# Strided and local attention before a bilinear feed-forward layer: local heads from batch 2 on with probabilities as weights, rows turned by DMA

## The chip, the core and the metric

The kernel runs on one core of one Trainium2 chip. The metric is the device time of one execution in microseconds (us). Before the change the median of three executions is 328.6 us (328.22 to 328.73). Times inside the kernel are taken from one profiled execution and count from the start of its span.

## What is computed

Eight batches of eight heads, 576 positions of 64 numbers each. Heads 0 to 3 attend locally (the last 32 positions), heads 4 to 7 attend to every 32nd earlier position. The head outputs of a position lie side by side and make one row of 512 numbers; the 4608 rows go through a bilinear feed-forward layer.

```python
mask_local = (rel >= 0) & (rel < stride)
mask_strided = (rel >= 0) & (pos[None, :] % stride == pos[:, None] % stride)
masks = np.stack([mask_local if h < H // 2 else mask_strided for h in range(H)], axis=0)
scores = np.where(masks[None, :, :, :], scores, -1000000000.0)
scores = scores - np.max(scores, axis=-1, keepdims=True)
attn = np.exp(scores)
attn = attn / (np.sum(attn, axis=-1, keepdims=True) + 1e-09)
return np.matmul(attn, v).astype(np.float32)
...
x = np.ascontiguousarray(attn_out.transpose(0, 2, 1, 3)).reshape(B * S, H * D)
...
a = x @ w_a
b = x @ w_b
return (a * b @ w_out).astype(np.float32)
```

## The kernel before

**The feed-forward layer sets the rhythm.** The rows are cut into nine tiles of 512. A tile has 16 slots, numbered through as `16 t + n`. In slots 0 to 11 (`ffn_ab`) TensorE forms 128 columns of `x @ w_a` and `x @ w_b`, eight matmuls of 512 columns (L603); ScalarE copies the first product out of PSUM (L620) and VectorE multiplies the two into `pf` (L623, L625). In slots 12 to 15 the tile is multiplied with `w_out`: plainly in tiles 0 and 1 (`ffn_y`, L755, a ScalarE copy at L764), and in tiles 2 to 8 by a scheme of seven half-size products (`ffn_ys` and `y_plan`, L691). There the products follow one another in `Y_ORDER`, six matmuls for each entry; the three PSUM banks X, Y and Z are accumulated on by several products, and ScalarE copies a bank out in between (`y_post`, L668). Thus product "1" is copied out of bank X before product "6" goes on adding to that bank; between them TensorE has the two entries of product "7", twelve matmuls.

**The left operand.** `xT` holds the rows turned, 128 features on the partitions in four chunks (chunks 0 and 1 are the local heads, 2 and 3 the strided ones), for four batches in a ring. Tile t reads the first columns of batch t, so batch b has to stand in `xT` when slot 16 b begins. In its first slot a tile takes chunks 0, 1 and 2 first and chunk 3 last (tile 1 leaves chunk 1 for last).

**Attention is woven in between.** The steps of batch b from 1 on are put at slots by the tables `STEPS` (batches 1 and 2), `LATER` and `IN_Y` (3 to 7), counted from slot 16 (b - 1). `S` is a unit of scores (L385), its exponential on ScalarE (L406) and its mask on VectorE (L424). `V` is a unit of outputs. A batch has eight units, 0 to 3 local and 4 to 7 strided; a unit is half of the positions of two heads. What stands at a whole number n runs behind the slot's own work, what stands at n - 0.5 runs in its middle. The order of every engine's instructions is this written order.

**Two forms of V.** Batches 0 and 1 use the probabilities as weights and the values, with a column of ones behind them, as the moving operand (`V_p`, L463). That gives rows with positions on the partitions; VectorE takes the reciprocal of the sums (`V_r`, L471) and multiplies (`V_n`, L486), and TensorE turns the rows by transposes (`step_X`). From batch 2 on (`FIRST_D`) `step_VT` uses the values as weights, with 64 columns of ones behind them, and the probabilities as the moving operand (L507). This gives the outputs turned already, and the sums in 64 partitions; ScalarE takes the logarithm (L516) and the exponential of its negative (L517), and VectorE multiplies straight into `xT` (L521 local, L523 strided). The ones are set by `fill_v`, a memset on GpSimd.

**Queues.** Loads go over GpSimd's queue. SyncE's queue has the stores of the results and the transfers that place the turned q and k of the next batch (`step_D`, L341 and L345). ScalarE's queue issues one transfer in all, a last piece of the output (L657).

Of the kernel before, what the change touches and what calls it, by code (L numbers as in the profile page):

```python
# [8 lines left out]
BF16 = mybir.dt.bfloat16  # L9
# [5 lines left out]
FIRST_D = 2  # L15
RL = 6
RS = 8
# [4 lines left out]
LW = 96  # L22
# [8 lines left out]
def kernel(  # L31
# [10 lines left out]
    nc = tc.nc  # L42
    B, H, S, D = q.shape
# [9 lines left out]
    HL = H // 2  # L53
# [5 lines left out]
    sb = ctx.enter_context(tc.tile_pool(name="sb", bufs=3))  # L59
    fsb = ctx.enter_context(tc.tile_pool(name="ffn", bufs=2))  # L60
    pst = ctx.enter_context(tc.tile_pool(name="pst", bufs=1, space=bass.MemoryType.PSUM))
    dram = ctx.enter_context(tc.tile_pool(name="dram", bufs=2, space=bass.MemoryType.DRAM))
# [18 lines left out]
    vl_buf = [const.tile([128, HL * 6, VW], BF16, name=f"vl{i}") for i in range(2)]  # L81
# [76 lines left out]
    XR = 4  # L158
    xT = const.tile([128, KD, XR * S], BF16)
# [11 lines left out]
    def fast_w(n, gs):  # L171
        a, b = ((wov[:, 0, 1], wov[:, 0, 0]), (wov[:, 1, 1], wf[:, 0]), (wov[:, 1, 1], wov[:, 0, 1]),
                (wov[:, 1, 0], wf[:, 1]))[n]
        nc.vector.tensor_tensor(wf[:, n, gs], a[:, gs], b[:, gs], op=ALU.subtract)
# [3 lines left out]
    def blocks(nm, z):  # L178
        z = int(z)
        return sb.tile([128, 2, (S, RS * GP)[z]], BF16, tag=f"t{nm}{z}", name=f"t{nm}{z}", bufs=1)  # L180
# [84 lines left out]
    def by_row(t):  # L265
        return t.rearrange("p (r h d) -> p h r d", h=2, d=D)

    def pair_up(nm, c):

        if (nm, c) == ("k", 1):  # L270
            t = shared[1][:96, -RL * 128:]
        else:
            t = blocks(*{"k0": "q0", "q0": "q1", "q1": "k0"}[f"{nm}{c}"])
            t = t.rearrange("p h n -> p (h n)")[:96, :RL * 128]
        nc.vector.tensor_copy(by_row(t), nats[1, nm, False][:, 2 * c:2 * c + 2])
        paired[1, nm, c] = t.rearrange("p (r m) -> p r m", r=RL)
# [85 lines left out]
    def unit(u):  # L362

        c, half = u // 2, u % 2
        return (c, half, 128, LW, 3) if c < 2 else (c, half, NP, NP, 4)
# [68 lines left out]
    xn = {}  # L434

    def V_p(b, u):
        c, half, M, n, G = unit(u)
        p = ps.pop((b, u))
        if b == 0:

            o = psum4["o"].tile([128, 512], F32, tag="o", name="o")
            if c < 2:
                of = o[:, :2 * G * (D + 1)].rearrange("p (j g e) -> p j g e", j=2, e=D + 1)
                sm = of[:, :, :, D:]
            else:
                of = o.rearrange("p (j g e) -> p j g e", j=2, e=D)
                sm = psum4["sum"].tile([128, 2, 4, 1], F32, tag="sum", name="sum")
        else:
            o = psum4["o"].tile([128, 2, 512], F32, tag="o", name="o")
            of = o[:, :, :G * (D + 1)].rearrange("p j (g e) -> p j g e", e=D + 1)  # L450
            sm = of[:, :, :, D:]
        for i in range(G):
            for j in range(2):
                if c < 2:
                    vt = vl_buf[b % 2][:, (2 * c + j) * 6 + 3 * half + i, 0:D + 1]
                elif b == 0:
                    r = 2 * i + j
                    vt = nats[0, "v", c - 2][:NP, half, r * D:(r + 1) * D]
                else:
                    vt = vs_buf[b % 2][:, 2 * (c - 2) + half, 2 * i + j, 0:D + 1]  # L460
                w = vt.shape[1]
                pt = p_cols(b, p, j, i, n, 128)[:M]
                nc.tensor.matmul(of[:, j, i, :w], lhsT=pt, rhs=vt, start=True, stop=True)  # L463
                if b == 0 and c >= 2:
                    nc.tensor.matmul(sm[:, j, i], lhsT=pt, rhs=vl_buf[0][:M, 0, D:D + 1], start=True, stop=True)
        held[b, "o", u] = of[:n, :, :, :D], sm[:n]

    def V_r(b, u):
        c, half, M, n, G = unit(u)
        rc = sb.tile([128, 2, 4], F32, tag="rc", name="rc")  # L470
        nc.vector.reciprocal(rc[:n, :, :G].unsqueeze(3), held[b, "o", u][1])  # L471
        held[b, "rc", u] = rc

    def V_n(b, u):
        c, half, M, n, G = unit(u)
        ov, _ = held.pop((b, "o", u))
        rc = held.pop((b, "rc", u))
        if (b, c // 2) not in xn:
            x = sb.tile([128, RS * 4 * D], BF16, tag="xr", name="xr", bufs=2)
            xn[b, c // 2] = x[:n, :S // n * 4 * D].rearrange("p (g h d) -> p g h d", h=4, d=D)  # L480
        x = xn[b, c // 2][:, :, 2 * (c % 2):2 * (c % 2) + 2, :]
        if c < 2 or b >= FIRST_D:
            dst = x[:, G * half:G * half + G].rearrange("p g j d -> p j g d")
        else:
            dst = x[:, :, half, :].rearrange("p (g j) d -> p j g d", j=2)
        nc.vector.tensor_mul(dst, ov, rc[:n, :, :G].unsqueeze(3).to_broadcast([n, 2, G, D]))  # L486

    def step_V(b, u):
        if b >= FIRST_D:
            step_VT(b, u)  # L490
            return
        V_p(b, u)
        V_r(b, u)
        V_n(b, u)

    def step_VT(b, u):

        c, half, M, n, G = unit(u)
        p = ps.pop((b, u))
        o = psum4["o"].tile([128, 2, 512], F32, tag="o", name="o")  # L500
        for i in range(G):
            for j in range(2):
                if c < 2:
                    vt = vl_buf[b % 2][:, (2 * c + j) * 6 + 3 * half + i]
                else:
                    vt = vs_buf[b % 2][:, 2 * (c - 2) + j, 4 * half + i]
                nc.tensor.matmul(o[:, j, i * n:(i + 1) * n], lhsT=vt, rhs=p_cols(b, p, j, i, n, n)[:M], start=True, stop=True)  # L507

        r = sb.tile([128, RS * 4 * D], BF16, tag="xr", name="xr", bufs=2)[:64, :4 * W].bitcast(F32)
        r = r.rearrange("p (j w) -> p j w", j=2)  # L510
        if c < 2:
            sums = o[64:, :, :W]
        else:

            sums, r = (t.rearrange(e, p=NP) for t, e in ((o[64:, :, :W], "d j (g p) -> d j p g"), (r, "d j (p g) -> d j p g")))
        nc.scalar.activation(r, sums, ACT.Ln)  # L516
        nc.scalar.activation(r, r, ACT.Exp, scale=-1.0)  # L517
        for j in range(2):
            dst = xT[64 * j:64 * j + 64, c, S * (b % XR):S * (b % XR + 1)]
            if c < 2:  # L520
                nc.vector.tensor_mul(dst[:, W * half:W * (half + 1)], o[:64, j, :W], r[:, j])  # L521
            else:
                nc.vector.tensor_mul(dst.rearrange("d (p r) -> d p r", r=RS)[:, :, G * half:G * (half + 1)],  # L523
                                     o[:64, j, :W].rearrange("d (g p) -> d p g", p=NP), r[:, j])
# [21 lines left out]
    def step_X(b, c):  # L546
# [15 lines left out]
    STEPS = {1: {5.5: "Tk2", 6: "Tq2", 7: "S4 Tk3", 7.5: "S5", 8: "Tq3", 8.5: "V4", 9: "S6 V5 Pk0", 9.5: "S7 Pq0",  # L562
# [4 lines left out]
    LATER = {-1: "S0", 0: "S1", 1: "V0", 2: "S2", 3: "V1", 4: "S3", 5: "V2", 6: "S4", 7: "V3", 8: "S5", 9: "V4", 10: "S6",  # L567
             11: "V5"}
    IN_Y = {2: "S7", 6: "V6", 11: "V7"}
    FN = {"Tk": step_Tk, "Tq": step_Tq, "S": step_S, "V": step_V, "X": step_X, "W": lambda b, n: fast_w(n, slice(0, 3)),  # L570
          "s": S_px, "m": S_m, "L": lead_vl, "Pk": lambda b, c: pair_up("k", c), "Pq": lambda b, c: pair_up("q", c),
          "Z": lambda b, n: zero_qz(0, nc.vector, ((1, 1),)), "D": lambda b, n: step_D(FIRST_D, 0, "k", n)}

    def run(b, slot):
# [209 lines left out]
    with tc.manual_schedule(engines={ENG.PE, ENG.SP, ENG.Pool, ENG.DVE, ENG.Activation}):  # L784
# [11 lines left out]
        for x, src in ((raw[0], k), (raw[1], q)):  # L796
            nc.sync.dma_start(out=x[:96].rearrange("p (h r d) -> p h r d", h=2, d=D),
                              in_=src[0, 0:2].rearrange("h (p r) d -> p h r d", r=RL))
# [62 lines left out]
        for b in range(1, B):  # L861
            for pos, names in (STEPS.get(b) or {16 * (b - 1) + x: n for x, n in LATER.items()}).items():
                steps.setdefault(pos, []).append((b, names.split()))
# [6 lines left out]
        def do(i, fn, *args):  # L870
            at.setdefault(i, []).append(lambda: fn(*args))

        soon = {}
        for t in FAST_Y[:-1]:
            soon[16 * t + 10] = [lambda t=t: fast_s(t, 2, slice(4, 6))]
            soon[16 * t + 11] = [lambda t=t, n=n: fast_s(t, n, slice(4, 6)) for n in (0, 1)]
        do(0, fill_v, vl_buf[0])
        do(0, fill_v, vs_buf[0])
        for c in range(4):
            do(0, load_wo, c)  # L880
# [25 lines left out]
        for i, jz in ((2, (0, 0)), (3, (1, 0)), (0, (0, 1))):  # L906
            do(i, zero_qz, 0, nc.vector, (jz,))
        do(14, rezero, 1)
        do(27, fill_v, vl_buf[1])
        do(28, fill_v, vs_buf[1])  # L910
        for n, slot in enumerate((16, 16, 19, 20)):
            do(slot, fast_w, n, slice(3, 6))
# [50 lines left out]
```

## Time and profile before

| what | value |
|---|---|
| median of three executions | 328.6 us |
| the profiled execution | 328.45 us |
| its span in the trace | 326.6 us |
| granted TensorE clock | 1.0 throughout |
| local units in the form of L507 | 24 (6 batches of 4), 144 matmuls of 96 columns |
| ScalarE's Ln and Exp (L516, L517) for all 48 units | 31.1 us and 32.8 us |
| VectorE's multiplies of the local units (L521) | 48 of 450 ns |
| GpSimd's memsets of the values' ones (L109) | 2 of 1.4 us and 2 of 1.8 us |

Busy times of an engine say little where instructions overlap: a matmul's record holds its latency, while the next one begins much sooner. The pace is read from the start of one group of matmuls to the start of the next.

### The profile page before, as it was taken

The numbers are of one execution on the slowest core, as the hardware profiler recorded it, in microseconds if no ns is written. First come the engines' busy times: TensorE is split into PE (matmuls) and PEld (weight loads), VectorE is DVE, ScalarE is ACT, GpSimd is POOL, SyncE is SP. The second block draws the span as 40 slices with busy tenths as digits, with TensorE's granted clock in tenths as the row PEclk, the third lists the DMA queues.
The fourth block names the chain that finished last, engine by engine and source line by source line (L and its number), as shares of the span: only waits on it lengthen the run. The fifth ranks groups of instructions, "written<-read, shape, count | busy, mean of one in ns | idle before, by whom it ended". The sixth has DMA issues, their size and how long they took to land.

```text
span 326.6 us, 7290 instructions
## 1 busy us (share of the span) xinstructions
PE 321.0 (98%) x2624; PEld 205.4 (63%) x2624; DVE 251.0 (77%) x530; ACT 210.1 (64%) x345; POOL 150.9 (46%) x280
## 2 busy tenths in 40 slices
PE   8999999999999999999999999999999999999994
PEld 6754555455555587557999885569555954584474
DVE  6766888889778989799879988998878645626652
ACT  6763775478778876887677767786777743323341
POOL 8845839599866554664475346643011001100000
PEclk9999999999999999999999999999999999999999
DMA  9999999999999799989898959897032040004004
GB/s 154 149 204 202 204 184 181 167 178 134 140 209 119 87 95 83 95 221 101 82 84 202 130 63 102 160 172 83 20 90 101 2 129 0 2 0 131 0 0 130
DMA packets 98724, 37.48 MB, mean 115 GB/s; under 512 B 76672, under 2 KB 95744, under 8 KB 98688
## 3 DMA queue, kind: packets, MB, share of 16 engines
q0 software_dynamic: 85968, 19.48, 64.2%
q1 hardware_dynamic: 12576, 17.47, 18.4%
q8 instruction: 21, 0.34, 0.4%
q14 instruction: 15, 0.12, 0.1%
q10 hardware_dynamic: 144, 0.07, 0.1%
HBM read 39.51 MB, written 9.44 MB: 150 GB/s over the span
## 4 chain that ended last, share of the span: by engine, by line
PE 93%; POOL 2%; DMA 2%; DVE 1%; ACT 0%; issue 0%; POOLq 0%
PE mm L603 55%; PE mm L691 17%; PE mm L755 6%; PE st L385 4%; PE o L507 4%; DMA vl<-in_v_dram 2%; PE mm L720 2%; POOL shared L196 1%; PE o L463 1%; PE end L720 1%; PE ab L603 1%; PE tp L532 1%; POOL vl L224 0%; PE tp L286 0%; PE tp L295 0%
## 5 line engine op out<-in xcount | busy, mean ns | idle before, releaser
L603 PE MATMUL mm<-xT,wa_sb 128*128 128x512 bf16 (+1 forms) x472 | 110.3, 357 | 0.0
L603 PE MATMUL mm<-xT,wb_sb 128*128 128x512 bf16 (+1 forms) x472 | 110.3, 357 | 0.0
L620 ACT COPY a_sb<-mm 128x512 f32<-128x512 f32 x106 | 62.1, 586 | 45.4 <-PE mm L603 44.7
L929 POOL CAST pace<-pf 1x1 f32<-1x1 bf16 x87 | 24.5, 281 | 113.4 <-DVE pf L623 108.5
L603 PEld LDWEIGHTS <-wb_sb 128*128 128x128 bf16 x480 | 46.4, 98 | 44.3 <-DMA wb_sb<-in_moe_w_b_dram 0.5
L623 DVE TENSOR_TENSOR pf<-a_sb,mm 128x512 bf16<-128x512 f32 x84 | 57.0, 679 | 18.6 <-PE mm L603 14.2
L603 PEld LDWEIGHTS <-wa_sb 128*128 128x128 bf16 x480 | 44.0, 98 | 31.2
L516 ACT ACTIVATE xr<-o 64x576 f32<-64x576 f32 x48 | 31.1, 648 | 22.6 <-PE o L507 22.3
L406 ACT ACTIVATE p<-st 72x576 bf16<-72x576 f32 (+1 forms) x56 | 36.4, 650 | 4.0 <-PE st L385 3.6
L517 ACT ACTIVATE xr<-xr 64x576 f32<-64x576 f32 x48 | 32.8, 683 | 1.5
L521 DVE TENSOR_TENSOR xT<-o,xr 64x288 bf16<-64x288 f32 x48 | 21.6, 450 | 13.3 <-ACT xr L517 12.6
L523 DVE TENSOR_TENSOR xT<-o,xr 64x288 bf16<-64x288 f32 x48 | 21.4, 446 | 11.7 <-ACT xr L517 11.1
L691 PEld LDWEIGHTS <-ps 128*128 128x128 bf16 x288 | 28.0, 98 | 3.1
L668 ACT COPY y_sb<-mm 128x512 f32<-128x512 f32 (+1 forms) x28 | 15.6, 556 | 17.9 <-PE mm L691 14.5
L691 PE MATMUL mm<-wf,ps 128*128 128x256 bf16 x216 | 25.5, 273 | 0.0
L755 PE MATMUL mm<-wo_sb,pf 128*128 128x512 bf16 x96 | 23.4, 379 | 0.0
L242 POOL DMA_DIRECT2D vs<-in_v_dram x24 | 19.6, 818 | 5.0 <-PE mm L691 2.4
L691 PEld LDWEIGHTS <-pf 128*128 128x128 bf16 x216 | 20.3, 98 | 2.5 <-issue 0.2
L691 PE MATMUL mm<-wo_sb,pf 128*128 128x256 bf16 x144 | 18.5, 273 | 0.1
L625 DVE TENSOR_TENSOR pf<-a_sb,mm 128x512 bf16<-128x512 f32 x22 | 14.9, 677 | 4.5 <-ACT a_sb L620 2.7
L211 POOL DMA_DIRECT2D kl<-in_k_dram x24 | 16.0, 665 | 5.1 <-issue 3.2
L211 POOL DMA_DIRECT2D ql<-in_q_dram x24 | 16.0, 665 | 5.0 <-DMA wo_sb<-in_moe_w_out_dram 3.9
(146 smaller groups left out, 453.6 us busy)
## 6 DMA issues: line engine op xcount, KB each, us to landing
out_dram<-y_sb SPq DMA_DIRECT2D x12, 512.0 KB, 5.5
out_dram<-y_sb SPq DMA_DIRECT2D x11, 256.0 KB, 3.4
vl<-in_v_dram POOLq DMA_DIRECT2D x6, 384.0 KB, 6.7
kl<-in_k_dram POOLq DMA_DIRECT2D x24, 72.0 KB, 2.9
ql<-in_q_dram POOLq DMA_DIRECT2D x24, 72.0 KB, 3.1
vs<-in_v_dram POOLq DMA_DIRECT2D x24, 72.0 KB, 3.4
wo_sb<-in_moe_w_out_dram POOLq DMA_DIRECT2D x4, 384.0 KB, 9.3
natk<-in_k_dram POOLq DMA_DIRECT2D x20, 72.0 KB, 3.3
```

The costliest lines, as they stand in the source:

```text
L211: nc.gpsimd.dma_start(out=t[32 * h:32 * h + 32], in_=src[b, h].rearrange("(i y) d -> y i d", y=32))
L406: nc.scalar.activation(p_flat(p)[:M, :2 * W].rearrange("p (i n) -> p i n", n=2 * n), st[:M].rearrange("p a (i n) -> p (a i) n", n=256)[:, ...
L516: nc.scalar.activation(r, sums, ACT.Ln)
L517: nc.scalar.activation(r, r, ACT.Exp, scale=-1.0)
L521: nc.vector.tensor_mul(dst[:, W * half:W * (half + 1)], o[:64, j, :W], r[:, j])
L523: nc.vector.tensor_mul(dst.rearrange("d (p r) -> d p r", r=RS)[:, :, G * half:G * (half + 1)], o[:64, j, :W].rearrange("d (g p) -> d p g", ...
L603: nc.tensor.matmul(ps_[:, c0:c0 + n], lhsT=w[:, kk, 128 * f:128 * (f + 1)], rhs=xT[:, kk, x0:x0 + n], start=(kk == first and c0 == 0), sto ...
L620: nc.scalar.copy(a_sb, ab[0])
L623: nc.vector.tensor_mul(pf[:, f, :].rearrange("p (i a s) -> p a i s", i=2, s=16), halves(a_sb), halves(ab[1]))
L691: nc.tensor.matmul(bank[b][:, q], lhsT=lhs(g, q), rhs=rhs(g), start=k in "172" and q == 0 and g == 0, stop=g == FG - 1, skip_group_check=True)
L755: nc.tensor.matmul(ybank[j], lhsT=pf[:, f, 128 * j:128 * (j + 1)], rhs=wo_sb[:, f], start=(f == 0), stop=(f == FD - 1))
L929: nc.gpsimd.tensor_copy(pace, done)
```

## The change

For the local units (u below 4) from batch 2 on, the outputs are made as in batches 0 and 1: `V_p`, `V_r` and `V_n`, into a tile `xl` of 96 partitions with 6 rows of 256 numbers each. The rows of a batch then go to a scratch tensor in DRAM by one transfer (`rows_out`, step "O"), which ScalarE's queue issues for batch 2 and SyncE's queue for the later ones. Two transfers with transposition read it back, one for each chunk of 128 features, into `xT` (`rows_in`, step "I"); ScalarE's queue issues both. `O0` stands at slot 27 for batch 2 and at 16 (b - 1) + 7 for the others; `I0` and `I1` stand at 29 and 29.5 (behind V6 of that place), and at 16 (b - 1) + 11 (behind V5) and 11.5. The strided units keep `step_VT`. The columns of ones of the local values are no longer filled beyond the single one that `consts` sets.

```diff
@@ -476,7 +476,10 @@
         if (b, c // 2) not in xn:
-            x = sb.tile([128, RS * 4 * D], BF16, tag="xr", name="xr", bufs=2)
+            if b >= FIRST_D:
+                x = sb.tile([128, RL * 4 * D], BF16, tag="xl", name="xl", bufs=1)
+            else:
+                x = sb.tile([128, RS * 4 * D], BF16, tag="xr", name="xr", bufs=2)
@@ -486,12 +489,25 @@
-        if b >= FIRST_D:
+        if b >= FIRST_D and u >= 4:
             step_VT(b, u)
             return
         V_p(b, u)
         V_r(b, u)
         V_n(b, u)
+
+    scratch = {}
+
+    def rows_out(b, _):
+
+        scratch[b] = dram.tile([S, HL * D], BF16, tag="xd", name="xd")
+        (nc.scalar if b == FIRST_D else nc.sync).dma_start(out=scratch[b].rearrange("(g p) e -> p g e", p=LW),
+                                                           in_=xn.pop((b, 0)).rearrange("p g h d -> p g (h d)"))
+
+    def rows_in(b, c):
+
+        nc.scalar.dma_start(out=xT[:, c, S * (b % XR):S * (b % XR + 1)], in_=scratch[b][:, 128 * c:128 * (c + 1)],
+                            transpose=True)
@@ -562,13 +578,13 @@
-             2: {20: "S0", 20.5: "S1", 21.5: "V0", 22: "S2", 23: "V1", 23.5: "S3", 24.5: "V2", 25: "S4", 26: "V3", 26.5: "S5",
-                 27.5: "V4", 28: "S6", 28.5: "V5", 29: "S7", 29.5: "V6", 30.5: "V7"}}
-    LATER = {-1: "S0", 0: "S1", 1: "V0", 2: "S2", 3: "V1", 4: "S3", 5: "V2", 6: "S4", 7: "V3", 8: "S5", 9: "V4", 10: "S6",
-             11: "V5"}
+             2: {20: "S0", 20.5: "S1", 21.5: "V0", 22: "S2", 23: "V1", 23.5: "S3", 24.5: "V2", 25: "S4", 26: "V3", 26.5: "S5", 27: "O0",
+                 27.5: "V4", 28: "S6", 28.5: "V5", 29: "S7 I0", 29.5: "V6 I1", 30.5: "V7"}}
+    LATER = {-1: "S0", 0: "S1", 1: "V0", 2: "S2", 3: "V1", 4: "S3", 5: "V2", 6: "S4", 7: "V3 O0", 8: "S5", 9: "V4", 10: "S6",
+             11: "V5 I0", 11.5: "I1"}
@@ -874,7 +890,6 @@
-        do(0, fill_v, vl_buf[0])
         do(0, fill_v, vs_buf[0])
...
-        do(27, fill_v, vl_buf[1])
         do(28, fill_v, vs_buf[1])
```

More of the change, by code (lines that the diff above doesn't have):

```diff
@@ L564 @@
                  12.6: "S1", 12.75: "L0 X2", 13: "s2 X3 V0 m2 L1 W3", 13.5: "V1 S3", 14: "V2 X0", 14.5: "V3 D1", 15: "X1"},
[2 rows of a table removed]
-    LATER = {-1: "S0", 0: "S1", 1: "V0", 2: "S2", 3: "V1", 4: "S3", 5: "V2", 6: "S4", 7: "V3", 8: "S5", 9: "V4", 10: "S6",
-             11: "V5"}
[2 rows of a table added]
+    LATER = {-1: "S0", 0: "S1", 1: "V0", 2: "S2", 3: "V1", 4: "S3", 5: "V2", 6: "S4", 7: "V3 O0", 8: "S5", 9: "V4", 10: "S6",
+             11: "V5 I0", 11.5: "I1"}
     IN_Y = {2: "S7", 6: "V6", 11: "V7"}
     FN = {"Tk": step_Tk, "Tq": step_Tq, "S": step_S, "V": step_V, "X": step_X, "W": lambda b, n: fast_w(n, slice(0, 3)),
-          "s": S_px, "m": S_m, "L": lead_vl, "Pk": lambda b, c: pair_up("k", c), "Pq": lambda b, c: pair_up("q", c),
+          "s": S_px, "m": S_m, "L": lead_vl, "O": rows_out, "I": rows_in, "Pk": lambda b, c: pair_up("k", c), "Pq": lambda b, c: pair_up("q", c),
           "Z": lambda b, n: zero_qz(0, nc.vector, ((1, 1),)), "D": lambda b, n: step_D(FIRST_D, 0, "k", n)}
```

## The prediction

> **What bounds the kernel now.** I read the page's busy shares and its chain of waits first, then the order of time of TensorE and ScalarE around the places that the change touches, and last the rows of transfers. The first two say who holds the time:
>
> ```profile
> PE 321.0 (98%) x2624; PEld 205.4 (63%) x2624; DVE 251.0 (77%) x530; ACT 210.1 (64%) x345; POOL 150.9 (46%) x280
> PE 93%; POOL 2%; DMA 2%; DVE 1%; ACT 0%; issue 0%; POOLq 0%
> ```
>
> TensorE is the bound. From about 20 us on, its groups follow one another without a hole worth naming, so the time changes in two ways only: TensorE has less to do, or something now keeps it waiting. ScalarE is 0% of the chain: work taken from it is worth nothing by itself, but a delay put on it is worth whatever TensorE then waits.
>
> **Removed from TensorE.** In the order of time, the start of a group against the start of the next gives its pace. The old form, then the form that the change puts in its place (from batch 1, which has it already):
>
> ```profile
> 68.79 0.42 PE L507 MATMUL o<-p,vl 128*128 128x96 bf16 x6
> 69.05 1.03 PE L603 MATMUL mm<-xT,wb_sb 128*128 128x512 bf16 x4
> ```
>
> ```profile
> 51.78 0.34 PE L463 MATMUL o<-vl,p 128*128 128x65 bf16 x6
> 51.96 0.41 PE L385 MATMUL st<-qz1l,kT1l 128*128 128x192 bf16 x3
> ```
>
> A unit of six matmuls takes 0.26 us with 96 moving columns and 0.18 to 0.20 us with 65 (four groups: 0.19, 0.18, 0.20, 0.18; mean 0.19). The gain is 0.07 us a unit, times 24 units: **-1.7 us**, all on the path. If the weight loads, which are now the masked probabilities, came late, nothing of it would be left; a unit of scores stands at least two slots (some 4 us) ahead of its outputs, so I keep the 1.7, with 0 as its other end.
>
> **Removed from ScalarE and VectorE.** Per local unit ScalarE loses a Ln and an Exp (0.65 + 0.68 us), 24 x 1.33 = 32 us in all. VectorE has 2 x 0.45 us replaced by these two:
>
> ```profile
> L486 DVE TENSOR_TENSOR xr<-o,rc 96x384 bf16<-96x384 f32 x8 | 4.3, 547 | 0.2
> L471 DVE RECIPROCAL rc<-o 96x6 f32<-96x6 f32 x8 | 1.5, 190 | 2.4 <-PE o L463 2.3
> ```
>
> That is 0.74 for 0.90 us, 24 x 0.16 = 4 us less. I cost both at nothing: TensorE covers them, having waited for neither. The one stall that I see at the head of a product stage (184.35 to 184.65 us, behind L623 of VectorE) might shrink; it is worth 0.3 us at most. GpSimd's two memsets of 1.4 us on the values also go; only the pacing and the loads stand behind them, and the loads have slack: nothing.
>
> **Added: the rows out.** One transfer of 576 rows of 512 bytes a batch. For batch 2, ScalarE issues it at slot 27, between its copy that ends at 81.03 us and its Ln at 82.06 us; an issue of 0.66 us fits this idle time. For the others SyncE issues it at slot 7. In tile 4, the tightest, the k transfers ahead of it end at 179.8 us and SyncE is next busy at 183.72 us, so it goes out at about 180 us and lands by 183.4 us with the 3.4 us of the 256 KB row below; ScalarE wants it at 185.9 us. Cover 2.5 us; no cost.
>
> **Added: two transposing transfers a batch, on ScalarE's queue.** This is the step that matters. The trace has no transfer with transposition. The nearest rows are these, the first with the duration of an issue, the others with the time to landing:
>
> ```profile
> L657 ACTq DMA_DIRECT2D out_dram<-y_sb x1: 655/655/655, 322.5 to 322.5; - x1
> ```
>
> ```profile
> out_dram<-y_sb SPq DMA_DIRECT2D x11, 256.0 KB, 3.4
> ...
> shared<-in_k_dram POOLq DMA_DIRECT2D x5, 144.0 KB, 5.6
> ...
> out_dram<-y_sb SPq DMA_DIRECT2D x1, 128.0 KB, 2.6
> ```
>
> Let T be the time for which one such issue keeps ScalarE, and L its time to landing (one moves 576 x 128 x 2 bytes, 144 KB). L lies between 2.6 and 5.6 us by these rows; I take 4.4, about half way between 3.4 and 5.6, since loads and q and k transfers run beside it. T is bounded below by 0.66, and above by the whole landing, 5.6, if the queue takes a transposition no faster than it is carried out. The nearest row is the issue on the same queue, and a transposition can hardly have fewer pieces than a plain copy: I take **T = 1.0**, that row and half as much again.
>
> What is queued behind them in batches 3 to 7? `I0` follows V5's Exp, and `I1` (middle of slot 12) comes before the copy of product "1", so both issues stand in one row ahead of that copy. Tile 2, ScalarE and TensorE in order of time:
>
> ```profile
> 116.43 0.65 ACT L516 ACTIVATE xr<-o 64x576 f32<-64x576 f32 x1 [0.54 <-PE o L507]
> 117.11 0.68 ACT L517 ACTIVATE xr<-xr 64x576 f32<-64x576 f32 x1
> 117.82 0.59 ACT L668 COPY y_sb<-mm 128x512 f32<-128x512 f32 x1
> 118.30 0.65 ACT L406 ACTIVATE p<-st 72x576 bf16<-72x576 f32 x1
> ```
>
> ```profile
> 117.79 2.78 PE L691 MATMUL mm<-wf,ps 128*128 128x256 bf16 x24
> 120.41 0.43 PE L507 MATMUL o<-p,vs 72*128 72x72 bf16 x8
> ```
>
> The copy starts 30 ns after the Exp, without idle time. TensorE's 24 matmuls take 2.62 us, 0.109 each; the first twelve are product "7" and the thirteenth adds to the bank that the copy reads: 117.79 + 1.31 = 119.10. The copy ends at 118.41. The cover is 0.7 us, and TensorE waits 2T - 0.7. Tiles 3, 5 and 6 show the same gap; in tile 4 the copy has another 0.25 us of idle time, so 0.97 there. Behind it, S7's exponential (until 118.95) has to pass VectorE's mask before V6's matmuls at 120.41: 118.95 + 0.45 leaves 1.0, less strict than the first. Sum for five batches: 10T - (4 x 0.7 + 0.97) = 10T - 3.8, at T = 1.0 **+6.2 us**; 2.8 at T = 0.66 and 52 at T = 5.6.
>
> Do they land in time? `I1` is issued at 117.8 + T; tile 3 wants chunk 1 at about 126.8 + (2T - 0.7), over 9 us later at T = 1. Hidden up to L of about 9.
>
> **Batch 2 has less room.** Its issues stand around V6 in the plain product stage of tile 1:
>
> ```profile
> 87.04 0.65 ACT L406 ACTIVATE p<-st 72x576 bf16<-72x576 f32 x1
> 88.27 0.65 ACT L516 ACTIVATE xr<-o 64x576 f32<-64x576 f32 x1 [0.58 <-PE o L507]
> 88.95 0.68 ACT L517 ACTIVATE xr<-xr 64x576 f32<-64x576 f32 x1
> ...
> 92.47 0.81 PE L603 MATMUL mm<-xT,wa_sb 128*128 128x512 bf16 x3
> ```
>
> The last of these lines is TensorE's first group of tile 2. `I0` goes at 87.69 and holds ScalarE to 88.69, V6's Ln and Exp end 0.4 us later than before, at 90.05; then `I1`. With L = 4.4 it lands at 94.45. TensorE wants chunk 1 at 92.47 + 0.22 = 92.69: **+1.8 us**, between 0 (T 0.66, L 2.6: it lands at 92.3) and 3.0 (L 5.6).
>
> **The sum.** -1.7 + 6.2 + 1.8 = +6.3 us on the profiled execution of 328.45 us (it lies 0.15 under the median, its span at 326.6): **334.7 us**.
>
> One rule speaks against the change. The Trainium skill (VectorE: DVE Perf Modes, "The three transpose paths") puts a 128x128 bf16 transposition at 1309 ns by DMA against 390 ns on TensorE. No row here shows the first. As an estimate from that page, 4.5 such blocks a transfer would be 5.9 us, both in a row 11.8; then chunk 1 would also come late in batches 3 to 7, by some 2 us each, and the sum would be near 347 us. The same skill (DMA: Bandwidth & Descriptors, "Latency and other measured facts") gives transposing transfers 261 GB/s, by which 144 KB are an estimated 0.6 us and the landing would be like a plain copy's; the forecast is nearer to this one.
>
> **The rivals.**
>
> *The issue is hidden (other side).* ScalarE's sequencer might issue while the Exp ahead is still running, since the transfers do not depend on it. Then 0.68 us of the two issues are covered, and with the 0.7 of the copy nothing is lost up to T = 0.69. For it: nothing in the two transfers waits for the Exp. Against: the only issue on ScalarE here, at 322.52, begins after the activation before it has ended (322.23), which decides nothing. Batch 2 would then be late by 0 to 1.3. Time 328.45 - 1.7 = 326.8, or up to 328.1 with batch 2 late.
>
> *The issue is long.* If the queue builds the transposition piece by piece, ScalarE becomes the bound at the head of every product stage. From T = 1.5 on I count it as this case: T = 2.5 gives 25 - 3.8 + 3 - 1.7 = +22.5, 351 us; the bound of 5.6 gives over 380. For it: 576 rows against the 128 of an output store. Against: SyncE's issues take about 0.6 us whatever their shape.
>
> *All landings late.* At T = 1 this decides from L over 9: at L = 12, 5 x 2.7 more, and batch 2 late by 90.05 + 12 - 92.69 = 9.4: 328.45 - 1.7 + 6.2 + 13.5 + 9.4 = 356 us. Against: no transfer of this size takes over 5.6 us beside the same loads.
>
> *The change does not do what it says*: the units keep 0.26 us, because weight loads set the pace. That alone would bring 336.4 us; the four groups of batch 1 speak against it.
>
> **Chances and range.** Forecast (T from 0.7 to 1.5, including the units' rival) 0.48; issue hidden 0.25; issue long 0.19; landings late 0.08. The forecast's own range is 330 to 341 (T 0.7 to 1.5, batch 2 between 0 and 3, rounded). The range over the cases is 326.6 to 350; above it lie half of the long issues and of the late landings, below it hardly anything. A difference of under 0.2% (0.66 us) can't be told from no change. Faster than that needs the hidden issue and batch 2 in time: 0.16. Within it: 0.09. Slower: 0.75.
>
> **What would show it.** Each step has a place in the changed profile: groups of L463 at 0.19 us from batch 2 on; ScalarE's issue row of the transposing transfers with T; a hole of TensorE of 2T - 0.7 before the third entry of product stage of tiles 2 to 6, put down to ScalarE's L668 copy; a wait of the first L603 of tile 2 for a transfer into `xT`. The forecast is wrong if TensorE shows no hole at the third entry, or if its holes are at the heads of tiles 3 to 7.

## The result, and the profile after

The changed kernel takes **339.36 us** (median of four executions, 337.54 to 340.98) against 328.67 us (328.22 to 329.6) before it on the same chip: a ratio of 1.032, with an interval of 1.026 to 1.038. It is slower. The predicted time was 334.7 us and its range 326.6 to 350. The profiled execution is the fastest of the four: 337.54 us, with a span of 335.7, so that between the two profiled spans (326.6 before) 9.1 us have to be found.

Line numbers are 16 higher from L507 on (`V_n`'s L486 is L489): the tile's matmuls L603 are L619 now, the product stage's L691 is L707, its copy L668 is L684; `V`'s L507, L516 and L517 are L523, L532 and L533. The transfers into `xT` are L509.

First the page's busy shares and its chain of waits, as before:

```profile
PE 318.6 (95%) x2597; PEld 203.2 (61%) x2624; DVE 246.5 (73%) x530; ACT 178.0 (53%) x297; POOL 149.1 (44%) x278
PE 81%; DMA 7%; ACTq 3%; DVE 3%; ACT 3%; issue 2%; SPq 1%; DVEq 0%
```

ScalarE gave up 32.1 us of busy time (210.1 to 178.0) and the kernel became longer. TensorE's share of the chain fell from 93% to 81%, and what came in is above all DMA, from 2% to 7%; ScalarE's queue, ScalarE and VectorE have 3% each. Where TensorE stood still is told by the list of what it waited for (the engine and line that waited, what ended the wait, us in total, how often, the longest):

```profile
PE mm L707 <- ACT y_sb L684: 7.2, 5, 1.9
PE o L523 <- DVE xT L539: 2.2, 1, 2.2
...
PE mm L619 <- DMA xT<-xd: 0.6, 1, 0.6
PE tp L286 <- ACT shared L837: 0.4, 1, 0.4
```

None of these four is in the same list of the kernel before. Five waits for the copy of product "1" are the predicted holes; the next two belong to batch 2. The last lies at the kernel's start; L286 waits there in `b3` and `b3_one` below as well, which leave batch 2 alone, and for 0.6 us in `v_only`, which has none of the transfers. So the transfers don't explain it.

**The holes.** Tile 2 in order of time, TensorE and then ScalarE, after the change (start, duration, engine and line, what it does; in brackets the idle time before it and what ended that):

```profile
120.15 1.47 PE L707 MATMUL mm<-wf,ps 128*128 128x256 bf16 x12
122.92 1.47 PE L707 MATMUL mm<-wf,ps 128*128 128x256 bf16 x12 [1.29 <-ACT y_sb L684]
```

```profile
119.47 0.68 ACT L533 ACTIVATE xr<-xr 64x576 f32<-64x576 f32 x1
119.53 2.63 ACTq L509 DMA_TRANSPOSE xT<-xd  x2
122.28 0.59 ACT L684 COPY y_sb<-mm 128x512 f32<-128x512 f32 x1 [2.13 <-PE mm L707]
```

The first twelve matmuls are product "7"; the next should begin 12 x 0.109 = 1.31 us later, at 121.46, and begin at 122.92, 1.46 late (1.29 of it is idle, since the record of the first twelve holds their latency). ScalarE explains it: its two issues stand in one row from 119.53 to 122.16, and the copy follows at 122.28. The issues begin 0.06 us after the Exp has *begun*, not after it has ended. The bracket behind the copy names TensorE, which had been done for long: ScalarE was held by the issues, and that is read from the line above, not from the bracket. Tiles 3 to 6 have idle times of 1.38, 1.48, 1.88 and 1.14 at the same place.

In tiles 3 to 5 the first issue comes later behind the Exp's start, because `I0` waits there until its rows have landed in DRAM. Tile 4, and the row of the transfers out on SyncE's queue (KB each, median us from issue to landing):

```profile
190.04 0.68 ACT L533 ACTIVATE xr<-xr 64x576 f32<-64x576 f32 x1
190.43 2.75 ACTq L509 DMA_TRANSPOSE xT<-xd  x2
```

```profile
xd<-xl SPq DMA_DIRECT2D x5, 288.0 KB, 6.4
```

The rows of tile 4 were sent at 183.95 us and landed 6.4 us later, at 190.35. `I0` went at 190.43, 0.39 us behind the Exp's start in place of 0.06. In tiles 3 and 5 it went 0.23 and 0.57 us behind it, after landings of 6.6 and 7.2 us; in tile 6 again 0.07. Over the three tiles this is 1.0 us, and they are the ones with the longest holes.

The line's own row gives an issue its price (duration in ns, least, median, most):

```profile
L509 ACTq DMA_TRANSPOSE xT<-xd x12: 1144/1234/1377, 88.9 to 262.6; - x12
...
DMA to landing us min/median/max: 2.7/4.7/5.7
```

**Batch 2.** ScalarE from 86 to 93 us:

```profile
86.63 0.65 ACT L406 ACTIVATE p<-st 72x576 bf16<-72x576 f32 x1
88.90 1.22 ACTq L509 DMA_TRANSPOSE xT<-xd  x1
90.22 0.65 ACT L532 ACTIVATE xr<-o 64x576 f32<-64x576 f32 x1 [2.94 <-issue]
...
92.02 1.19 ACTq L509 DMA_TRANSPOSE xT<-xd  x1
```

An issue that needs nothing more stands idle on ScalarE from 87.28 (the end of L406) to 88.90, and the second, behind V6's Exp, until 92.02. TensorE pays twice:

```profile
92.58 0.43 PE L523 MATMUL o<-p,vs 72*128 72x72 bf16 x8 [2.16 <-DVE xT L539]
...
95.33 0.38 PE L619 MATMUL mm<-xT,wa_sb 128*128 128x512 bf16 x1 [0.56 <-DMA xT<-xd]
```

First V7 waits until V6 has passed ScalarE and VectorE, then tile 2 waits for chunk 1. What the second issue waited for is in the chain of waits, followed back from there (start, duration, what):

```profile
86.05 5.95 DMA kT1l<-tk
...
92.02 3.28 DMA xT<-xd
```

It is a transfer of SyncE's queue, issued at 86.05, that places the turned k of batch 3: data with which batch 2's rows have nothing to do. In the built program the transfers of SyncE's and ScalarE's queues share eight completion counters in turn, in the order in which they are written, and a transfer is not sent before the last one on its counter has landed. The trace's records of the issues, which name the counters, bear this out. `I0` waits for the counter of a transfer into `qz1l` that was issued at 83.50 and landed at 88.82, 0.08 us before `I0` went; `I1` shares with the one shown, which landed at 91.99. The rows were not what `I0` waited for: sent at 80.29, they had landed by 84.8.

**The gain** is there too. The unit of L507 shown before took 0.26 us; in its place:

```profile
68.67 0.34 PE L463 MATMUL o<-vl,p 128*128 128x65 bf16 x6
68.85 1.03 PE L619 MATMUL mm<-xT,wb_sb 128*128 128x512 bf16 x4
```

It is 0.18 us from start to start, 0.08 less. The account of the 9.1 us: the holes 7.2 idle and some 0.17 more each by the starts, 8.0; batch 2, 2.16 + 0.56 = 2.7; the start 0.4; less 1.7 of shorter outputs: 9.4.

### The profile page after: what moved, and what is told of

The parts are those of the page before. It is cut to its first block, busy times and chain, and to the rows that moved or that the text cites. A ratio compares the mean times of both kernels' runs of the same rounds, so it can differ in the third digit from the quotient of the medians.

```text
span 335.7 us, 7209 instructions
## 1 busy us (share of the span) xinstructions
PE 318.6 (95%) x2597; PEld 203.2 (61%) x2624; DVE 246.5 (73%) x530; ACT 178.0 (53%) x297; POOL 149.1 (44%) x278
## 4 chain that ended last, share of the span: by engine, by line
PE 81%; DMA 7%; ACTq 3%; DVE 3%; ACT 3%; issue 2%; SPq 1%; DVEq 0%
PE mm L619 51%; PE mm L707 13%; PE st L385 3%; PE mm L771 3%; ACTq L509 3%; PE o L463 2%; DMA kT1l<-tk 2%; DMA xT<-xd 2%; PE mm L736 2%; PE o L523 2%; DMA raw<-in_q_dram 1%; PE end L736 1%; DMA qz0s<-tq 1%; SPq L345 1%; DMA qz0l<-tq 1%
## 5 line engine op out<-in xcount | busy, mean ns | idle before, releaser
L619 PE MATMUL mm<-xT,wb_sb 128*128 128x512 bf16 (+1 forms) x468 | 109.9, 357 | 0.5
L619 PE MATMUL mm<-xT,wa_sb 128*128 128x512 bf16 (+1 forms) x453 | 108.5, 356 | 1.3 <-DMA xT<-xd 0.6
L619 PEld LDWEIGHTS <-wb_sb 128*128 128x128 bf16 x480 | 46.3, 98 | 44.2 <-DMA wb_sb<-in_moe_w_b_dram 0.3
L619 PEld LDWEIGHTS <-wa_sb 128*128 128x128 bf16 x480 | 43.6, 98 | 32.1 <-issue 0.8
L406 ACT ACTIVATE p<-st 72x576 bf16<-72x576 f32 (+1 forms) x56 | 36.4, 650 | 19.0 <-PE st L385 18.8
L539 DVE TENSOR_TENSOR xT<-o,xr 64x288 bf16<-64x288 f32 x48 | 21.4, 446 | 19.6 <-ACT xr L533 19.2
L707 PEld LDWEIGHTS <-ps 128*128 128x128 bf16 x288 | 28.0, 98 | 11.1 <-issue 8.0
L707 PE MATMUL mm<-wf,ps 128*128 128x256 bf16 x216 | 26.3, 272 | 7.2 <-ACT y_sb L684 7.2
L684 ACT COPY y_sb<-mm 128x512 f32<-128x512 f32 (+1 forms) x28 | 15.5, 554 | 26.4 <-PE mm L707 16.3
L771 PE MATMUL mm<-wo_sb,pf 128*128 128x512 bf16 x93 | 23.1, 379 | 0.2
L532 ACT ACTIVATE xr<-o 64x576 f32<-64x576 f32 x24 | 15.5, 647 | 12.0 <-PE o L523 9.0
L707 PEld LDWEIGHTS <-pf 128*128 128x128 bf16 x216 | 20.3, 98 | 2.6 <-issue 0.2
L424 DVE TENSOR_TENSOR p<-p,mask_s 72x576 int16<-72x576 int16 x28 | 12.5, 448 | 8.4 <-ACT p L406 8.3
L707 PE MATMUL mm<-wo_sb,pf 128*128 128x256 bf16 x144 | 18.5, 273 | 0.1
L653 DVE TENSOR_TENSOR ps<-pf 128x512 bf16<-128x512 bf16 (+1 forms) x48 | 17.7, 380 | 0.4
```

What stands on the lines that cost most here:

```text
L406: nc.scalar.activation(p_flat(p)[:M, :2 * W].rearrange("p (i n) -> p i n", n=2 * n), st[:M].rearrange("p a (i n) -> p (a i) n", n=256)[:, ...
L619: nc.tensor.matmul(ps_[:, c0:c0 + n], lhsT=w[:, kk, 128 * f:128 * (f + 1)], rhs=xT[:, kk, x0:x0 + n], start=(kk == first and c0 == 0), sto ...
L653: nc.vector.tensor_tensor(s[:, n], a, b, op=op)
L707: nc.tensor.matmul(bank[b][:, q], lhsT=lhs(g, q), rhs=rhs(g), start=k in "172" and q == 0 and g == 0, stop=g == FG - 1, skip_group_check=True)
L771: nc.tensor.matmul(ybank[j], lhsT=pf[:, f, 128 * j:128 * (j + 1)], rhs=wo_sb[:, f], start=(f == 0), stop=(f == FD - 1))
```

## The experiments

The theory after the result: the holes of tiles 2 to 6 are the price of two issues ahead of one copy, fixed for each issue, and batch 2 loses by waits of its own. Rivals: the price goes with the rows or bytes; the matter is the landings; or something else of the change (the rows out, VectorE's new work) costs. Each run has its own runs of the kernel before beside it; ratios are against these.

### Without the rows coming in, and without the rows going out either

`no_in` leaves out the two transfers into `xT` (the local chunks of batches 2 to 7 then aren't renewed; half of them is set to zero once), `v_only` the rows out as well.

```diff
-                 27.5: "V4", 28: "S6", 28.5: "V5", 29: "S7 I0", 29.5: "V6 I1", 30.5: "V7"}}
+                 27.5: "V4", 28: "S6", 28.5: "V5", 29: "S7", 29.5: "V6", 30.5: "V7"}}
...
-             11: "V5 I0", 11.5: "I1"}
+             11: "V5"}
```

In `v_only` the steps `O0` go too.

> The changed kernel without the two transposing transfers; the rows still go out to DRAM. The local heads' chunks of the left operand are not renewed from batch 2 on (a memset on GpSimd at slot 10 fills the ring's places of batches 2 and 3 once). Theory A (the two issues hold ScalarE ahead of the copy of product 1, and batch 2's V6 and landing wait on them; nothing else costs): all holes vanish and the shorter outputs remain, 328.6 - 1.7 = 326.9 us. Theory B (the rows' way out, or VectorE's new steps, cost too): above 328.6 us. Theory C (the shorter moving operand saves nothing in place): 328.6 us.

> As the run without the transposing transfers, and without the transfer to DRAM as well: the outputs in their new form alone. The local heads' chunks are not renewed from batch 2 on. Theory A: 326.9 us, the same as with the rows going out within 0.3 us, since the transfer out is covered. Theory B with the price in the transfer out: lower than the run with it by that price.

`no_in`: 327.2 us against 328.77, ratio 0.996 (0.9945 to 0.998). `v_only`: 327.65, ratio 0.996 (0.9945 to 0.998). So the shorter outputs are worth 1.6 us by the medians of `no_in` and 1.7 by its span (324.9 against 326.6). `v_only` shows less, 1.1 and 0.7 (its span is 325.9); two waits ahead of batch 2 that `no_in` doesn't have (0.6 us at L286, 0.4 for `wb_sb`) are 1.0 us of its span. The rows out by themselves cost nothing that can be told, and all of the loss comes with the two transfers into `xT`. The list of TensorE's waits of `no_in` has none of the four lines above.

### I1 at another place

`i1_late` issues `I1` of batches 3 to 7 behind the copy of product "7", `i1_v6` behind V6 of the product stage.

```diff
-             11: "V5 I0", 11.5: "I1"}
-    IN_Y = {2: "S7", 6: "V6", 11: "V7"}
+             11: "V5 I0"}
+    IN_Y = {2: "S7", 4: "I1", 6: "V6", 11: "V7"}
```

For `i1_v6` the last line is `IN_Y = {2: "S7", 6: "V6 I1", 11: "V7"}`.

> The changed kernel with I1 of batches 3 to 7 moved from the middle of slot 12 to behind the copy of product 7 (behind the fourth entry of the product stage). Theory A: one issue of 1.24 us ahead of the copy of product 1 is covered by the Exp (0.62) and by the 0.7 of TensorE's twelve matmuls, the other by ScalarE's idle time behind the copy of product 7. The five holes (7.2 us by the waits, some 8 by the starts) go, batch 2's 3 us stay: 339.4 - 8 = 331.4 us. Theory B (the transfers' landings or their load on the queues set the loss, wherever they are issued): 339 us.

> I1 of batches 3 to 7 behind V6 of the product stage, still later than in the run with I1 behind product 7. Theory D: there two holes stayed (tiles 4 and 5, 1.2 and 1.7 us) because I1 waited until a q transfer landed that shares its counter; by V6's Exp it has landed, and the issue lies beside this Exp and ScalarE's idle 0.87 us behind it. All five holes go: 335.3 - 3.6 = 331.7 us, batch 2's 3 us staying. If the issue's length alone made those two holes: 335 us. Price of lateness: if I1 lands over 3 to 4 us after its issue, tiles 3 to 7 wait at their head for it, up to 1 us each.

`i1_late` took 335.33 us against 328.77, ratio 1.020 (1.019 to 1.022): better than the change, but 4 us more than expected. The holes of tiles 2, 3 and 6 were gone; tiles 4 and 5 kept 1.20 and 1.68 us. The chain of waits of `i1_late` in tile 4 says why (start, duration, what):

```profile
190.06 3.02 DMA qz0l<-tq
...
193.10 1.23 ACTq L509
```

The copy before the issue had ended at 191.62. The issue stood until 193.10, for a transfer of SyncE's queue that places q, and the next copy stood behind it: the wait of batch 2 again, at a new place. The two holes are 2.9 of the missing 4 us. Part of it is also a slower clock. After the hole of 2.24 us in batch 2, this run's clock is lower in three stretches of 2 us. One of them, with the busy times of the engines; the last three figures are the granted TensorE clock, the DMA share and GB/s:

```profile
94.00:96.00 2.00, 2.00 (x7) 0.82 (x6) 0.60 (x2) 1.32 (x2) 1.54 (x3) 0.50 0.95 292
```

The stretches before and behind it have 0.84 and 0.81, and the changed kernel 1.00 in all three. By these figures the three stretches lose some 1.7 us (an estimate).

`i1_v6` came out as expected: 331.78 us against 329.03, ratio 1.008 (1.005 to 1.011). ScalarE in tile 2 of `i1_v6`:

```profile
120.10 1.24 ACTq L509 DMA_TRANSPOSE xT<-xd  x1
121.47 0.59 ACT L684 COPY y_sb<-mm 128x512 f32<-128x512 f32 x1 [0.74 <-PE st L385]
```

One issue alone holds the copy until 121.47, 0.75 us behind the Exp's end at 120.72, 0.62 of the issue lying beside the Exp, and that is about the cover of product "7" (0.7): TensorE has no hole in tiles 2 to 6. So the holes are the *second* issue's.

### Is the price per issue, per row or for transposing?

Three forms of the transfers, at the places of the change. `halves` cuts each into two of 288 rows; `one_issue` takes both chunks in one of 576 rows by 256 columns; `plain` moves the same 144 KB twice without turning them (what lands in `xT` is then not turned).

```diff
+        for i in range(2):
+            nc.scalar.dma_start(out=xT[:, c, S * (b % XR) + W * i:S * (b % XR) + W * (i + 1)],
+                                in_=scratch[b][W * i:W * (i + 1), 128 * c:128 * (c + 1)], transpose=True)
```

```diff
+        if c == 0:
+            nc.scalar.dma_start(out=xT[:, 0:2, S * (b % XR):S * (b % XR + 1)], in_=scratch[b][:, :], transpose=True)
```

```diff
+        nc.scalar.dma_start(out=xT[:, c, S * (b % XR):S * (b % XR + 1)],
+                            in_=scratch[b].rearrange("s e -> (s e)").rearrange("(c p n) -> c p n", c=2, n=S)[c])
```

> Each transposing transfer in two of 288 rows, four issues a batch for the same bytes. If an issue costs the same whatever its rows (1.24 us), four hold ScalarE for 5 us: each of the five holes grows by 2.5, batch 2 by 1.2 to 2.5, some 353 us. If an issue costs by its rows, 0.6 each, the time stays at 339 us. Theory A wants the time to follow the sum of the issues, B wants it to stay.

> Both chunks of a batch by one transposing transfer of 576 rows of 256 columns, at the place of I0; I1 goes. Two halves of a transfer took as long each as a whole one. If an issue costs the same whatever it moves (1.24 us), it is covered by the Exp and TensorE's twelve matmuls: no hole in tiles 2 to 6, batch 2 keeps 2 to 3 us: 327.2 + 2.5 = 329.7 us. If it costs by its columns or by blocks of 128 (2.5 us), the holes stay: 339 us.

> The two transfers back from DRAM without transposition: the same bytes, places, queue and order, plain copies of 128 rows of 1152 bytes (the local heads' chunks get the rows in a wrong order from batch 2 on). Theory A (the length of a transposing issue on ScalarE is the price): a plain issue is some 0.4 to 0.66 us, two of them 0.8 to 1.3, covered by the Exp (0.62) and the 0.7 of TensorE: the five holes of tiles 2 to 6 vanish. Theory D (in batch 2 the two transfers wait for a counter that a transfer of q and k of SyncE's queue still holds, whatever they are): batch 2's 2 to 3 us stay. Together 327.2 + 2 to 3 = 329 to 330 us. Theory B (any transfer back through DRAM costs this): 337 us or more.

Their issue rows, `halves`, `one_issue` and `plain` in turn:

```profile
L510 ACTq DMA_TRANSPOSE xT<-xd x24: 1122/1274/1547, 89.9 to 284.1; - x24
```

```profile
L510 ACTq DMA_TRANSPOSE xT<-xd x6: 1291/1324/1617, 91.7 to 259.4; - x6
```

```profile
L509 ACTq DMA_DIRECT2D xT<-xd x12: 326/330/647, 87.5 to 253.8; - x12
```

Half a chunk: 1.27 us. Four times as much: 1.32. One chunk, in the change: 1.23. The price is fixed for each issue, whatever is turned. The same bytes without turning cost 0.33. The times follow. `halves` took 362.51 us against 328.77, ratio 1.103 (1.096 to 1.111), nearer to the 353 of a fixed price than to the 339 of a price by rows, and beyond both. ScalarE in tile 2 of `halves`:

```profile
123.24 5.14 ACTq L510 DMA_TRANSPOSE xT<-xd  x4
```

Four issues in a row, the copy behind them at 128.50, and holes of 3.49 to 4.11 us in all five tiles, 19.0 together. What is beyond 353 is mostly the clock: it averaged 0.974 in the profiled execution, which over its span of 357.4 us is some 9 us (an estimate), and some groups of twelve matmuls behind the holes took 2.72 us in place of 1.47.

`plain` took 331.56 us against 329.03, ratio 1.008 (1.005 to 1.011), above the 329 to 330 that had been expected, with one hole of 0.32 us left in tiles 2 to 6. It still waited in batch 2 (0.38 and 1.09 us), where `I1` went out at 91.22 us: that wait needs no transposition. Its ten executions lie between 328.98 and 333.5, and the profile is that of the fastest, so some 2.6 us of the median are not in the trace.

`one_issue` took 335.19 us against 328.54, ratio 1.019 (1.017 to 1.022), between the 329.7 and 339 that had been expected, 5.5 us above the figure for a fixed price. Tiles 2 to 6 have no hole, as a fixed price has it. What remained is batch 2: its issue stood until 91.70 us for the transfer into `qz1l`, V7 came 2.27 us late, and then the clock fell, to 0.50 from 96 to 98 us. Six matmuls of L771 that take 1.46 us after the same hole in the changed kernel take 2.75 here, from 96.25 on. In this execution the clock is also low at 16 to 24 us, ahead of all that the change touches, so not all of its 335 us is batch 2's.

### Batch 2 by itself

`b3` makes the change for batches 3 to 7 alone; `b2_pool` is `i1_v6` with the transfers that place the local q and k of batch 3 on GpSimd's queue in place of SyncE's.

```diff
-        if b >= FIRST_D and u >= 4:
+        if b == FIRST_D or b > FIRST_D and u >= 4:
```

```diff
-                        nc.sync.dma_start(out=dst[:, PAD:] if z == 0 else dst[:, :RS * GP], in_=t[64 * c:64 * c + 64, e])
+                        (nc.gpsimd if (b, z) == (3, 0) else nc.sync).dma_start(out=dst[:, PAD:] if z == 0 else dst[:, :RS * GP], in_=t[64 * c:64 * c + 64, e])
```

(and the same in L345; in `b3` the steps O0, I0 and I1 of batch 2 go and its values' ones are filled as before).

> The change for batches 3 to 7 alone; batch 2 keeps the values as weights. Its 0.28 us of gain go, and with them the wait of V7 in tile 1 and the late landing at tile 2's head, by the waits 2.16 + 0.56 and by the starts of the groups 3.0 us: 339.4 - 2.7 = 336.7 us. If batch 2's loss is only moved (its holes come back in tile 2): 339.4 us.

> The run with I1 behind V6 (331.8 us), and the turned local q and k of batch 3 placed by GpSimd's queue instead of SyncE's. Theory D: batch 2's two transfers no longer share a counter with transfers in flight. I0 starts right behind S7's exponential (some 1.5 us sooner), V7's wait of 1.8 us in tile 1 goes; the landing of chunk 1 may still be late by up to 1 us: 331.8 - 1.8 = 330 us. Were the wait of I0 one for the rows on their way out, it would stay: 331.8 us. GpSimd has 12 more issues in this stage; if loads come late for it, the time rises instead.

`b3`: 334.79 us against 329.03, ratio 1.019 (1.015 to 1.023), 1.9 us under what was expected. The five holes stayed, 7.9 us in its list of waits, and batch 2's two waits went: 4.6 us less than the change. That is more than the 2.7 us of idle time, and what makes up the rest isn't shown.

`b2_pool`: 330.17 us against 328.54, ratio 1.006 (1.004 to 1.007), as expected. ScalarE around `I0` and `I1` of batch 2:

```profile
86.92 1.28 ACTq L509 DMA_TRANSPOSE xT<-xd  x1
...
89.10 1.16 ACTq L509 DMA_TRANSPOSE xT<-xd  x1
```

Both issues go out some 2 to 3 us earlier than in the change, the second 0.01 us behind the start of V6's Exp (89.09), and V7's wait is gone. The first even goes ahead of S7's exponential, which stands before it in the written order and begins at 87.18. What is left is a wait at the place where the prediction had put one, tile 2's first group:

```profile
93.47 0.59 PE L619 MATMUL mm<-xT,wa_sb 128*128 128x512 bf16 x2 [0.70 <-DMA xT<-xd]
```

It is for chunk 0, not for chunk 1 as forecast: `I0` took 6.5 us to land, at 93.43. The move takes batch 3's transfers off the shared counters and off SyncE's queue at once, so the run alone doesn't tell which of the two frees the issue. The records of the changed kernel speak for the counter: there each of the two issues waits for its counter and goes within 0.1 us of the landing that frees it.

### Is there a version that gains?

`b3_i1_v6` joins `b3` and `i1_v6`; `b3_one` joins `b3` and `one_issue`. Neither has a hole of the change left by the theory.

> Both of the last two edits: the change for batches 3 to 7, I1 behind V6. Theories A and D: no hole is left, the gain of five batches remains, 5 x 0.28 = 1.4 us: 328.7 - 1.4 = 327.3 us, up to 329 with what is left of small waits. If it stays above 330 us, something beside the issues and the shared counters costs.

> One transposing transfer a batch, batches 3 to 7 alone. With the fixed price of an issue: no hole, 5 x 0.28 us of gain: 328.8 - 1.4 = 327.4 us, as the run without transfers back (327.2) less batch 2's share. With a price by columns: 336 us, as the run of batches 3 to 7 with two transfers.

`b3_i1_v6`: 328.77 us against 329.03, ratio 0.999 (0.997 to 1.001). `b3_one`: 328.85 against 328.54, ratio 1.001 (0.999 to 1.003). Neither can be told from the kernel before. The gain of some 1.4 us that both expectations had at their centre doesn't show; the first had allowed for up to 329. The profile of `b3_one` has a span of 326.3 us, 1.4 over that of `no_in`; its waits account for 0.8 (0.4 at the start, 0.4 in front of one L707) and batch 2's four longer units for 0.3. The rest stays open.

## Why the prediction was right

The mechanism was right and the time lies in the range. Two terms of the sum were too small.

**Shorter outputs, -1.7 us: right.** `no_in` shows 1.6 in the medians and 1.7 in the spans, `v_only` 1.1 and 0.7 with two waits of its own. ScalarE's and VectorE's relief at nothing: right (32 us less on ScalarE, and no more gain than TensorE's). Rows out at nothing: right by themselves (`v_only` against `no_in`), but not ahead of the transfers in. The text had them land in 3.4 us, 2.5 us before they were wanted; in tiles 3 to 5 they took 6.4 to 7.2, and `I0` waited for them, 1.0 us together.

**Two issues ahead of the copy, +6.2 us: right in place and cause, too small.** The holes stand at the third entry of the product stages of tiles 2 to 6, put down to the copy, as the text said, and cost 8.0 us. T was taken as 1.0 and measured 1.23; by the prediction's formula 10T - 3.8 that makes 8.5. That this comes so near to 8.0 is partly luck, since the formula itself was off in two ways that nearly cancel. The rival that hides the issue had a true half: the first issue runs beside the Exp, for 0.62 us in tiles 2 and 6 and for 0.46, 0.29 and 0.12 in tiles 3 to 5, 2.1 us together, which the forecast counted as lost. Against it stand 1.1 us of gaps behind the issues, 0.4 of them a wait of `I1` for another transfer in tile 4, which no step had; and the ten issues together are 12.6 us, a little over ten medians. 12.6 + 1.1 - 2.1 - 3.8 = 7.8, of the 8.0 seen. In tile 2: two issues with their gaps 2.75, less 0.62, is a delay of 2.1 for the copy; less the cover of 0.7 that is the 1.4 us seen. For the rival to win, T would have had to be 0.69 or less; 0.33, a plain copy's, nearly does it, and `plain` has nearly no hole. That figure also lies under the 0.66 that the text took as the least an issue costs, from the one row that it had.

**Batch 2, +1.8 us: the step that was mis-sized, and by a route that it didn't have.** The landing was taken as 4.4 us and measured 4.7 in the median (3.3 for the one that counted). But `I0` was to go at 87.69 us and went at 88.90; `I1` was to go at 90.05 and went at 92.02. Both waited for transfers of another queue. The prediction asked whether an issue's data was ready and whether the engine was free, not what else the sent transfer had to wait for. The cost was 2.7 us in place of 1.8, most of it at V7, where nothing had been expected; with these waits out of the way (`b2_pool`) it is 0.7, and that for chunk 0.

These two terms, 1.8 and 0.9 us larger, bring 334.7 to 337.4; the profiled execution took 337.54. The median of the four is 1.8 us above it; two of the four executions had a mean clock of 0.995. That is no step of the prediction, and its cause isn't shown.

**The rule and the trace.** The text weighed the Trainium skill (VectorE: DVE Perf Modes, "The three transpose paths") with its 1309 ns for a block of 128x128 by DMA. Nine blocks in one transfer landed in 5.3 us (median of `one_issue`), where nine times that figure would be 11.8; four and a half landed in 4.7. The figure is not a rate at which the blocks add up here. By the medians the second chunk's 144 KB added 0.6 us to the landing, an increment of about 246 GB/s, near the 261 GB/s of the other page named (DMA: Bandwidth & Descriptors, "Latency and other measured facts"). But the landings of one form scatter by 3 us (2.7 to 5.7), and from half a chunk (3.7 in `halves`) to a whole one the medians differ by 1.0, so the agreement may be chance. Nor is the landing like a plain copy's, which the text drew from that rate: the same 144 KB landed in 2.7 us without turning (`plain`), in 4.7 with it.

The rivals: the long issue from 1.5 us on is excluded by the row (at most 1.38 in the change); late landings show nowhere in tiles 3 to 7; the units did take the shorter time.

## What to carry to other kernels

Work that a DMA takes off the bound engine has to be paid for on the queue that issues it: count each issue by its own duration at the place where it stands, and look which copy behind it frees a buffer of the bound engine. Fewer, larger transfers are better than two when the price is fixed for each: one issue fitted under the cover here, two did not, and four left 19 us of holes. The rows that such an issue reads have to be landed by then as well. And an issue whose data is ready may still wait for the landing of an unrelated transfer of another queue, so ask what the transfer waits for as well as what the data waits for.

## What the runs showed that had not been expected

- A transposing issue holds ScalarE for a fixed 1.23 to 1.32 us (288x128, 576x128 and 576x256 elements), a plain one of 144 KB for 0.33.
- An issue whose waits are over begins while the activation before it still runs: 0.06 us after the Exp's start in tile 2, and in `b2_pool` even 0.26 us ahead of the start of an exponential that stands before it in the written order.
- After holes of 2.24 and 2.27 us the granted clock fell to 0.50 for a stretch of 2 us; after one of 2.16 us in the changed kernel's profile it stayed at 1.00, and so it did after two of 3.81 and 3.70 us in `halves`. The Trainium skill (TensorE: Matmul & The Clock Gate, "Why this matters for your kernels") asks for "No PE-idle gaps >~3µs between matmul bursts"; here shorter ones were followed by the lower clock in two profiles, and longer ones in `halves` not always, so the length of the hole alone doesn't decide it. What does isn't shown.
